# A DeltaNet attention block and a SwiGLU FFN on one core: the first group's inverse in blocks of 16 rows, corrected on TensorE

## The chip, the core and the metric

The kernel runs on one NeuronCore of a Trainium2 chip (trn2). Its time is device microseconds of one execution, as the median of several runs. A profile is one execution of its own: it gives the span from the first to the last instruction, every engine's busy time, and the clock that was granted to TensorE. Everything is float32, except that the FFN's weights arrive as 64-bit floats and are turned into float32 in the kernel by operations on their words.

## The reference

A linear recurrence over the sequence (DeltaNet), for 4 batches of 8 heads with 768 positions of 48 elements, and then an FFN over all 3072 tokens (d_model 384, d_ff 1536).

```python
def _attn_ref(q, k, v, beta):                # each (4, 8, 768, 48); beta (4, 8, 768)
    k_n = k / (np.linalg.norm(k, axis=-1, keepdims=True) + 1e-06)
    state = np.zeros((B, H, D, D))
    for t in range(S):
        kt, vt, bt = k_n[:, :, t], v[:, :, t], beta[:, :, t, None]
        y[:, :, t] = np.einsum('bhd,bhde->bhe', q[:, :, t], state)
        v_old = np.einsum('bhde,bhd->bhe', state, kt)
        state = state + bt[..., None] * np.einsum('bhd,bhe->bhde', kt, vt - v_old)
    return y

def _moe_ref(x, w_gate, w_val, w_out):        # x: y as (3072, 384)
    g = x @ w_gate
    return (g / (1.0 + np.exp(-g)) * (x @ w_val)) @ w_out
```

## The kernel before

**Chunks.** The sequence is cut into 12 chunks of 64 positions, two chunks to a group. Within a chunk the recurrence becomes matrix products. With L the strictly lower part of the 64x64 gram matrix K K^T of a head and D the diagonal of beta over the squared norms, the updates u of a chunk solve a triangular system, (I + D L) u = D r. Here r is the (scaled) v minus what the state gives for the keys. The kernel builds Z, the inverse of I + D L times D, and takes u = Z r on TensorE. Then y = Q state + P u with P the masked gram matrix of Q and K, and the state grows by K^T u. The 32 heads of a chunk lie as 2 x 16: two on the partitions (64 rows each), 16 along the free axis.

**The inverse.** It is found by substitution on VectorE for 32-row diagonal blocks of both chunks of a group at once (`substitute`, lines 524 and 530: a multiply and an add for each of 31 steps). Two 32-row blocks make the 64 rows of a chunk. The block below the diagonal comes from a join on TensorE, -Z2 L21 Z1 (`join_late` for the first two groups, lines 634 and 646).

**Order of the work.** The order on every engine is written out by hand (`tc.manual_schedule`): an engine does its instructions in program order. Group 0 is special, since nothing can lie over it. Its grams (`first_gram`: diagonal blocks and the block below), its norms (`norms`, `first_n`), `first_scale`, the substitution and `join_late(0, 0, ...)` come before chunk 0 can go. Chunk 0 is carried in five steps by `advance(0)`: r; u (line 782, copied at 793); y (lines 804, 841, 843); x by transposes (853, 856); the state (816). With x of chunk 0 the FFN starts (`gate_val`, line 1052): two 128-column blocks of gate and val are a pair, f = 0, 2, ... 10, twelve matmuls with 256 tokens moving. The pairs of chunk 0 and chunk 1 follow; `point` puts a step of the recurrence in front of a pair, `fill` puts VectorE work behind one. For chunks 0 and 1 the FFN is plain. From chunk 2 on it runs in a form with fewer products (line 957 on), which the change doesn't touch.

**Weights.** They come in pieces of 128 rows (`stage`: 256 KB for 256 columns, 512 KB for 512). ScalarE takes the words apart (`power_step`, lines 262 and 268) and VectorE puts them together (`convert`, lines 279, 287, 299). A piece is staged in a place that has no other use at the time; conversion of a piece frees its place and issues the next load. The first 12 pieces have 256 columns and cover f = 0 and 2; 12 of 512 cover the rest of gate and val; 12 follow for `w_out`. `need(n)` says that a pair needs the first n pieces.

**Queues.** Nearly all loads and stores are issued by SyncE (SP), in program order: K, Q (`load_k`, `load_q`: four issues for a chunk, 64 rows x 8 heads x 48 elements, so pieces of 192 bytes), V (`load_v`: eight issues for a chunk), weights. The first halves of K of chunks 0 and 1 also use ScalarE's queue, half of beta GpSimd's.

Of the kernel before, what the change touches and what calls it, by code (L numbers as in the profile page):

```python
# [20 lines left out]
def kernel(  # L21
# [108 lines left out]
    def halves(x, c, bp, b):  # L130
        return x[2 * bp + b, :, c * C : (c + 1) * C, :]

    def load_k(c, dmas=(nc.sync,)):
        for n in range(2 * NB):
            bp, b = divmod(n, 2)
            dmas[n % len(dmas)].dma_start(
                out=kn_of(c)[64 * b : 64 * b + 64, bp, :, 0:D],
                in_=halves(k, c, bp, b).rearrange("h p d -> p h d"),
            )

    def load_q(c):
        for bp in range(NB):
            for b in range(2):
                nc.sync.dma_start(
                    out=qpad[c % QB][64 * b : 64 * b + 64, bp, :, 0:D],
                    in_=halves(q, c, bp, b).rearrange("h p d -> p h d"),
                )
# [28 lines left out]
    def load_v(c):  # L176
        vin[c] = work.tile([128, 2, NB, NJ, D], FP32, name="vin", bufs=2)
        for bp in range(NB):
            for b in range(2):
                src = halves(v, c, bp, b).rearrange("(j par) p d -> par p j d", par=2)  # L180
                for par in range(2):
                    s = 64 * (b ^ par)
                    nc.sync.dma_start(out=vin[c][s : s + 64, par, bp], in_=src[par])
# [11 lines left out]
    for f0, m in ((0, 256), (256, 256), (512, PIECE), (1024, PIECE)):  # L195
        for t in range(KT):
            for dst, src in ((wg_sb, moe_w_gate), (wv_sb, moe_w_val)):
                pieces.append((dst, src, t, f0, m))
# [22 lines left out]
    place_of += in_wo + in_z1 + in_wo + in_work + (in_z1 + in_work) * 3  # L221

    beta_s = places["wo"].bitcast(FP32)[:, 6 * H_ : 6 * H_ + NG * 128]
    LATE = {"zb": 0, "p_sb": 6}
# [13 lines left out]
    def stage(n):  # L238
# [11 lines left out]
        nc.sync.dma_start(  # L250
# [3 lines left out]
    def power_step(n):  # L254
# [3 lines left out]
        power = words(hp[10 + (n // 2 % 4 if n < N_HALF else (0, 2, 3, 1)[n % 4])])  # L258
# [11 lines left out]
    def convert(ns):  # L270
# [24 lines left out]
        for n in range(ns[-1] + 1, ns[-1] + 7):  # L295
            if n < min(N_HALF, len(pieces)) or ns[-1] + 3 > n < len(pieces):
                power_step(n)
# [15 lines left out]
    for b in range(2):  # L313
# [9 lines left out]
        )  # L323

# [51 lines left out]
    def load_beta(at, queue=nc.gpsimd):  # L376
# [5 lines left out]
            in_=beta.rearrange("(bp b) (j par) s -> b par bp j s", b=2, par=2)[  # L382
# [13 lines left out]
    def scale_v_heads(c):  # L396
        r = vin[c].rearrange("p par bp j d -> p (par bp j) d")
        for h in range(HH):
            nc.scalar.mul(r[:, h], r[:, h], n_t[c // 2][:, c % 2, h : h + 1])

    scaled = set()

    def scale_v(c):
        scaled.add(c)
        spent.append(1.4)
        r = vin[c].rearrange("p par bp j d -> p (par bp j) d")
        n = n_t[c // 2][:, c % 2, :, None].to_broadcast([128, HH, D])
        nc.vector.tensor_tensor(out=r, in0=r, in1=n, op=ALU.mult)

    def banks(name, tag):  # L410

        if tag == "ffn":
            return [ps_ffn([128, 512], name) for _ in range(2)]
        p = ps_pair(name, tag)
        return [p[:, 0], p[:, 1]]

    def turned(c, of_q, tag=None):

        tag = tag or ("py" if of_q else "px")
# [5 lines left out]
        if c >= blocks_of[of_q][1]:  # L425
            xt_v = xt.rearrange("p (bp b j i) -> p bp j b i", bp=NB, b=2, j=NJ)
# [19 lines left out]
    def gram_steps(c, of_q, tag=None, copies=(nc.vector.tensor_copy,) * 2):  # L446

        xt = (qt if of_q else kt)[c]
        p_g = banks("p_g", tag or ("py" if of_q else "px"))
# [47 lines left out]
    z1s, mbs = {}, []  # L497
    WAIT = "wait"
# [40 lines left out]
    first_of = {}  # L539

    def first_tiles():
# [4 lines left out]
        a_sb[0] = a[:, R * R :].rearrange("p (c h j) -> p c h j", c=2, h=HH)  # L546
        zb = work.tile([128, R, R], FP32, name="zb", bufs=1)
        nc.vector.memset(zb, 0.0)
        nc.vector.memset(ztp[0], 0.0)
        first_of["zb"] = zb  # L550

    def first_gram(c, tag):

        p_g = ps_pair("p_g", tag)
        p_v = p_g.rearrange("p par (x h i) -> p par x h i", x=2, i=R)
        for bp, j, par, b, _ in every():
            k_v = kt[c][half_of(par), bp, j, b].rearrange("p (x i) -> p x i", x=2)
            h, s_ = NJ * bp + j, b ^ par
            hi, lo = slice(64 * s_, 64 * s_ + R), slice(64 * s_ + R, 64 * s_ + C)
            nc.tensor.matmul(p_v[hi, par, 1, h], k_v[:, 0], k_v[:, 0])  # L560
            nc.tensor.matmul(p_v[lo, par, :, h], k_v[:, 1], k_v)
        return p_g, p_v

    def first_diag(c, par, p, copy):
        at = HH * c + HH // 2 * par
        copy(first_of["diag"][:, at : at + HH // 2], p[1][:, par, 1])

    def first_below(c, p):
        for lo in (slice(R, C), slice(64 + R, 64 + C)):
            nc.scalar.copy(  # L570
                a_sb[0][lo, c].rearrange("p (par h) j -> p par (h j)", par=2),
                p[0][lo, :, 0 : HH // 2 * R],
            )

    def first_scale(mb, r_b):
        zb, b = first_of["zb"], beta_b[:, 0]
        nb = work.tile([128, R], FP32, name="nb", tag="nb_1", bufs=1)
        for _ in range(2):
            nc.gpsimd.tensor_tensor(out=b, in0=b, in1=r_b, op=ALU.mult)
        nc.gpsimd.tensor_copy(zb.rearrange("p k i -> p (k i)")[:, 0 : R * R : R + 1], b)  # L580
        nc.vector.tensor_scalar_mul(nb, b, -1.0)
        nc.vector.tensor_tensor(
            out=mb, in0=mb, in1=nb[:, None, :].to_broadcast([128, R, R]), op=ALU.mult
        )
        return zb
# [7 lines left out]

    def turned_m(g, tag):

        a_v = a_of[g].rearrange("p (m i) -> p m i", i=C)
        p_m = banks("p_m", tag)
        half_r = R // 2
        for j in range(R):
            p = p_m[j // half_r][:, R * (j % half_r) : R * (j % half_r) + R]  # L600
            for quad, at in QUADS:
                nc.tensor.matmul(p[quad], a_v[quad, :, at + j], ident[quad, quad])
        return [
            (slice(half_r * n, half_r * n + half_r), p.rearrange("p (j i) -> p j i", i=R))
            for n, p in enumerate(p_m)
        ]
# [50 lines left out]
    def invert(g):  # L657
# [3 lines left out]
        if g > 1:  # L661
            mb = new_mb()
            yield from turn(mb.rearrange("p j i -> p i j"), a_v[:, R:C])
        else:
            mb = mbs.pop()
# [82 lines left out]
    def advance(c):  # L748
# [7 lines left out]
        p_y = recur(ps_pair("p_y", "py"))  # L756
        if c > 0:
            p_r = recur(ps_pair("p_r", "px"))
# [20 lines left out]
        yield  # L779
        p_u = recur(ps_pair("p_u", "px"))  # L780
        for bp, j, par, b, first in every():
            nc.tensor.matmul(  # L782
                p_u[half_of(b), par, bp, j],
                zt[half_of(b ^ par), par, bp, j],
                r[half_of(b ^ par), par, bp, j],
                start=first,
                stop=True,
                skip_group_check=True,
            )
        uu = work.tile([128, 2, NB, NJ, D], FP32, name="uu", tag="r", bufs=2)  # L790
        each = range(NB) if c == 0 else (slice(0, NB),)
        for bp in each:
            nc.scalar.copy(uu[:, :, bp], p_u[:, :, bp])
# [6 lines left out]
        pq = p_sb.pop(c)  # L800

# [38 lines left out]
        for bp in each:  # L840
            nc.scalar.copy(y[:, bp, :, 0], p_y[:, 0, bp])
            for b in range(2):
                nc.scalar.copy(y[half_of(b), bp, :, 1], p_y[half_of(1 - b), 1, bp])
# [201 lines left out]
    def gate_val(c, f, fill, within=None):  # L1045

        ps = {}
        for w_sb, name in ((wg_sb, "p_gate"), (wv_sb, "p_val")):
# [11 lines left out]
            if name == "p_gate":  # L1060
                nc.scalar.activation(sil, ps[name], ACTF.Silu)
                fill(2)
                if within is not None:
                    point(within)
        new_h(c, f, len(hs))
# [496 lines left out]
```

## Time and profile before

| | |
|---|---|
| median of 3 runs | 715.93 us (715.0 to 716.48) |
| profiled execution | 713.96 us, of which the span is 712.3 us |
| mean granted TensorE clock | 0.966 |
| TensorE matmul busy | 679.6 us (95% of the span) |
| VectorE, ScalarE, GpSimd busy | 475.6, 261.8, 53.8 us |
| first FFN matmul | at 62.37 us |
| DMA over the span | 62.57 MB, mean 88 GB/s |

All places in time are microseconds from the start of the span. A line number such as L524 is the line of the kernel that issued the instruction; in a row, `out<-in` names the tiles. One float32 matmul of the program is two records in the profile (a transpose is one), so "x12" of an FFN row is six matmuls. Matmul ends are modelled, so a busy TensorE isn't one at its peak; a granted clock of 0.5 means that it runs at half its rate. "issue" as the reason of a wait means that the profile shows nothing that was waited for.

### The profile page before, as it was taken

The numbers are of one execution on the slowest core, as the hardware profiler recorded it, in microseconds if no ns is written. First come the engines' busy times: TensorE is split into PE (matmuls) and PEld (weight loads), VectorE is DVE, ScalarE is ACT, GpSimd is POOL, SyncE is SP. The second block draws the span as 40 slices with busy tenths as digits, with TensorE's granted clock in tenths as the row PEclk, the third lists the DMA queues.
The fourth block names the chain that finished last, engine by engine and source line by source line (L and its number), as shares of the span: only waits on it lengthen the run. The fifth ranks groups of instructions, "written<-read, shape, count | busy, mean of one in ns | idle before, by whom it ended". The sixth has DMA issues, their size and how long they took to land.

```text
span 712.3 us, 25668 instructions
## 1 busy us (share of the span) xinstructions
PE 679.6 (95%) x11368; PEld 637.9 (90%) x11368; DVE 475.6 (67%) x1085; ACT 261.8 (37%) x555; POOL 53.8 (8%) x46
## 2 busy tenths in 40 slices
PE   4747999999999999999999999999999999999997
PEld 3636788866799999999999999999999999999997
DVE  5995765779799967888458888469854345333342
ACT  3557755312453343224333235233153043142230
POOL 8003000201300030000120000300000000000000
PEclk9556999999999999999999999999999999999999
DMA  7786444002753162166144166035142142121210
GB/s 149 173 230 171 128 112 131 26 12 45 206 111 80 40 119 67 26 136 133 29 97 105 25 125 123 18 97 113 24 112 71 24 99 60 47 68 46 67 46 22
DMA packets 144575, 62.57 MB, mean 88 GB/s; under 512 B 124400, under 2 KB 127472, under 8 KB 144464
## 3 DMA queue, kind: packets, MB, share of 16 engines
q1 hardware_dynamic: 141968, 60.36, 36.1%
q8 instruction: 89, 1.46, 0.8%
q10 hardware_dynamic: 2112, 0.39, 0.4%
q0 software_dynamic: 384, 0.17, 0.1%
q14 instruction: 22, 0.18, 0.1%
HBM read 53.82 MB, written 7.08 MB: 86 GB/s over the span
## 4 chain that ended last, share of the span: by engine, by line
PE 89%; DVE 5%; ACT 3%; issue 1%; DMA 1%; SPq 0%; DVEq 0%; ACTq 0%
PE ffn L957 42%; PE ffn L1160 19%; PE ffn L1052 9%; PE ffn L1077 4%; PE p_g L452 3%; PE p_s L816 2%; PE p_r L760 2%; PE p_u L782 2%; DVE tmp L524 2%; DVE zb L530 2%; PE p_y L769 1%; PE p_y L804 1%; PE p_f L853 1%; DMA kn<-in_k_dram 1%; PE p_j L723 1%
## 5 line engine op out<-in xcount | busy, mean ns | idle before, releaser
L957 PE MATMUL ffn<-x_ffn,wg_sb 128*128 128x128 f32 x840 | 128.3, 275 | 0.4 <-ACT x_ffn L856 0.2
L957 PE MATMUL ffn<-x_ffn,wv_sb 128*128 128x128 f32 x840 | 128.1, 275 | 0.0
L957 PEld LDWEIGHTS ffn<-x_ffn,wg_sb 128*128 128x128 f32 x840 | 111.1, 192 | 0.7 <-ACT ffn L1013 0.3
L957 PEld LDWEIGHTS ffn<-x_ffn,wv_sb 128*128 128x128 f32 x840 | 110.7, 192 | 0.0
L987 ACT ACTIVATE sil<-ffn 128x256 f32<-128x256 f32 x120 | 46.0, 383 | 131.9 <-PE ffn L957 126.8
L1160 PE MATMUL ffn<-wo_sb,h_f 128*128 128x192 f32 x480 | 83.4, 327 | 0.0
L992 DVE TENSOR_TENSOR h_f<-sil,ffn 128x256 f32<-128x256 f32 x120 | 49.6, 418 | 47.6 <-ACT sil L987 45.1
L1160 PEld LDWEIGHTS ffn<-wo_sb,h_f 128*128 128x128 f32 x480 | 78.1, 190 | 0.4
L1121 DVE TENSOR_TENSOR ffn<-ffn,p_sb 128x512 f32<-128x512 f32 x58 | 40.4, 696 | 44.6 <-ACT ffn L1013 43.5
L530 DVE TENSOR_TENSOR zb<-zb,tmp 128x31 f32<-128x31 f32 (+15 forms) x186 | 63.7, 343 | 6.4
L524 DVE TENSOR_TENSOR tmp<-zb,mb 128x31 f32<-128x31 f32 (+15 forms) x186 | 63.2, 340 | 5.2
L957 PE MATMUL ffn<-x_t,h_f 128*128 128x128 f32 x480 | 61.2, 280 | 0.1
L957 PEld LDWEIGHTS ffn<-x_t,h_f 128*128 128x128 f32 x480 | 56.2, 191 | 1.4 <-ACT ffn L970 0.3
L668 POOL TENSOR_TENSOR n_b<-mb,half 128x32 f32<-128x32 f32 x5 | 30.0, 5995 | 297.6 <-DVE mb L494 258.5
L1121 DVE TENSOR_TENSOR o_sb<-o_sb,ffn 128x192 f32<-128x192 f32 x49 | 17.2, 351 | 51.2 <-PE ffn L1160 49.1
L970 ACT COPY ffn<-ffn 128x512 f32<-128x512 f32 x30 | 17.1, 571 | 63.6 <-PE ffn L957 57.2
L1052 PE MATMUL ffn<-x_ffn,wg_sb 128*128 128x256 f32 x144 | 35.8, 401 | 0.9 <-ACT x_ffn L856 0.9
L1160 PE MATMUL ffn<-last_k,h_f 128*128 128x192 f32 x200 | 35.9, 327 | 0.0
L1052 PE MATMUL ffn<-x_ffn,wv_sb 128*128 128x256 f32 x144 | 33.4, 381 | 0.0
L1052 PEld LDWEIGHTS ffn<-x_ffn,wg_sb 128*128 128x128 f32 x144 | 28.3, 201 | 5.6 <-ACT x_ffn L856 1.4
L1160 PEld LDWEIGHTS ffn<-last_k,h_f 128*128 128x128 f32 x200 | 32.9, 190 | 0.0
L1052 PEld LDWEIGHTS ffn<-x_ffn,wv_sb 128*128 128x128 f32 x144 | 27.0, 190 | 3.7
(242 smaller groups left out, 1048.1 us busy)
## 6 DMA issues: line engine op xcount, KB each, us to landing
h_f<-w_s SPq DMA_DIRECT2D x60, 256.0 KB
p_sb<-w_s SPq DMA_DIRECT2D x27, 256.0 KB
vin<-in_v_dram SPq DMA_DIRECT2D x96, 48.0 KB
out_dram<-o_sb SPq DMA_DIRECT2D x48, 96.0 KB
kn<-in_k_dram SPq DMA_DIRECT2D x40, 96.0 KB
zt<-in_moe_w_out_dram SPq DMA_DIRECT2D x6, 384.0 KB
qpad<-in_q_dram SPq DMA_DIRECT2D x36, 64.0 KB
wo_sb<-in_moe_w_gate_dram SPq DMA_DIRECT2D x4, 512.0 KB
```

Source lines behind the costliest of these rows:

```text
L452: nc.tensor.matmul(p_v[par][half_of(b if of_q else b ^ par), bp, j], kt[c][half_of(par), bp, j, b], xt[half_of(par), bp, j, b],)
L524: nc.vector.tensor_tensor(out=t_v, in0=zb[:, 0 : j + 1, j : j + 1].to_broadcast([128, j + 1, m]), in1=mb[:, j : j + 1, j + 1 : R].to_broad ...
L530: nc.vector.tensor_tensor(out=zb[:, 0 : j + 1, j + 1 : R], in0=zb[:, 0 : j + 1, j + 1 : R], in1=t_v, op=ALU.add,)
L668: nc.gpsimd.tensor_tensor(out=n, in0=mb.rearrange("p j i -> p (j i)")[:, 0 : R * R : R + 1], in1=half, op=ALU.pow,)
L957: nc.tensor.matmul(p[:, u], w(u), moving, start=start and u == 0, stop=True, skip_group_check=True,)
L970: nc.scalar.copy(p_y, p_x)
L987: nc.scalar.activation(sil[:, n].rearrange("p (i n) -> p i n", i=2), p[:, 0:2], ACTF.Silu)
L992: nc.vector.tensor_tensor(out=h_of(c, f, j), in0=sil[:, n].rearrange("p (i n) -> p i n", i=2), in1=p[:, 2:4], op=ALU.mult,)
L1052: nc.tensor.matmul(ps[name][:, i], w_sb[:, t, (f + i) * 128 : (f + i + 1) * 128], xts[c][:, t], start=(t == 0 and i == 0), stop=(t == KT - 1),
L1077: nc.tensor.matmul(p_o, hs[c, f - f % 2][:, f % 2, bp * 128 : (bp + 1) * 128], wo_sb[:, f], start=(f == 0), stop=(f == FT - 1),)
L1121: nc.vector.tensor_tensor(out=out, in0=a, in1=b, op=ALU.add)
L1160: nc.tensor.matmul(p[x, part], a(f - f % 2)[:, f % 2], b(f), start=not begun and f == 0, stop=f == FH - 1, skip_group_check=True,)
```

## The change

The first group's inverse is made differently, and what hangs on it is put in another order.

- **Blocks of 16 rows.** The substitution of group 0 runs on 16-row diagonal blocks, the two of a 32-row part at once in one instruction: 15 steps. Nothing is joined. What results is Z for block-diagonal matrices of 16 rows.
- **Three rounds.** With L now the part below the 16-row blocks, N = -D' L (D' for Z of the blocks) is made on TensorE (`n_products`), and u follows from v0 = Z r by three times u = v0 + N u: products on TensorE, sum on VectorE. N has no entries but below the blocks, so three rounds are exact for four blocks. L is masked by ScalarE with per-row factors (`low_gram`, `low_copies`, and masks `m_rows`, `m_low`, made by VectorE from the identity); Z is spread from 16-row blocks to its places with masks too (`spread_z`).
- **Loads.** The batches that share a row pair are chosen differently (0 with 2 and 1 with 3 instead of 0 with 1 and 2 with 3), so that 16 heads of a half lie behind each other in memory: K and Q take two issues for a chunk, V four. The first two weight pieces go to ScalarE's queue, the others come behind Q0, K2, K3 and V0.
- **Pieces.** Gate and val have 24 pieces of 256 columns and 6 of 512; staging places and the pace of conversion change with them. Pieces 0 and 1 are converted beside the first norms.
- **Order.** v of chunks 0 and 1 is scaled on GpSimd. Q of chunk 1 and its gram come before the substitution ends. Chunk 1's chain (state, r, v0, three rounds, state, y, x) is put between the matmuls of the first two pairs, one step behind every three matmuls (`behind`). The inverse of group 1 begins after the first pair of chunk 1, with its own transposes on VectorE instead of TensorE's (`turned_m` goes).

The core of the diff:

```diff
-        for bp in range(NB):
-            for b in range(2):
-                nc.sync.dma_start(
-                    out=qpad[c % QB][64 * b : 64 * b + 64, bp, :, 0:D], ...
+    def load_heads(t, x, c, dmas=(nc.sync,)):
+        for b in range(2):
+            dmas[b % len(dmas)].dma_start(
+                out=t[64 * b : 64 * b + 64, :, :, 0:D].rearrange("p bp h d -> p (bp h) d"),
+                in_=halves(x, c, b).rearrange("bp h p d -> p (bp h) d"))
...
-    for f0, m in ((0, 256), (256, 256), (512, PIECE), (1024, PIECE)):
+    for f0, m in ((0, 256), (256, 256), (512, 256), (768, 256), (1024, PIECE)):
...
+    def low_gram(c, bank):
+        p_g = banks("p_g", bank)
+        ...
+        for bp, j, par, b, _ in every():
+            k_v = kt[c][half_of(par), bp, j, b]
+            nc.tensor.matmul(p_v[par][half_of(b ^ par), bp, j], k_v, k_v)
+        return p_g
+    def low_copies(c, p_g):
+        for par in range(2):
+            ...
+            for x in range(3):
+                at = slice(B16 * x, B16 * x + B16)
+                nc.scalar.mul(l_sb[c][:, HH // 2 * par : HH // 2 * (par + 1), at],
+                              p_h[:, :, at], m_low[:, x : x + 1])
...
+    def first_substitution():
+        zb, mb = pairs_of_blocks(first_of["zb"]), pairs_of_blocks(first_of["mb"])
+        for j in range(B16 - 1):
+            m = B16 - 1 - j
+            ...   # t_v: 2 * (j + 1) * m elements
+            nc.vector.tensor_tensor(out=t_v, in0=zb[...], in1=mb[...], op=ALU.mult)
+            nc.vector.tensor_tensor(out=z_v, in0=z_v, in1=t_v, op=ALU.add)
+    def spread_z(c, x, engine): ...          # 128 x 512, by engine
+    def n_products(c, p_n, bp):
+        for j in range(NJ):
+            for par, b in ORDER:
+                rows, h = half_of(b ^ par), HH // 2 * par + NJ * bp + j
+                nc.tensor.matmul(p_v[par][half_of(b), bp, j], l_sb[c][rows, h], zt[rows, h])
...
     def advance(c):
+        for bp in range(NB):
+            if c == 0:
+                n_products(c, p_n, bp)
+                n_copies(c, p_n, bp, nc.scalar.copy)
+            p_u_of(bp, lambda par, bp, j: zt[:, par, bp, j], r, lambda b, par: half_of(b ^ par))
+            if c == 0:
+                nc.scalar.copy(v0[:, :, bp], p_u[:, :, bp])
+        if c > 0:
+            nc.scalar.copy(v0, p_u)
+        uu = v0
+        if c < 2:
+            yield MORE
+            for n in range(3):
+                for bp in range(NB):
+                    p_u_of(bp, lambda par, bp, j: n_m[:, par, NJ * bp + j],
+                           uu if n else v0, lambda b, par: half_of(b))
+                    if c == 0:
+                        plus(uu[:, :, bp], v0[:, :, bp], p_u[:, :, bp])
+                if c > 0:
+                    plus(uu, v0, p_u)
+                    if n < 2:
+                        yield MORE
...
-        for n, _ in enumerate(substitute(mb, zb)):
-        ...
-        m_1 = turned_m(1, "ffn")
-        scale_v_heads(0)
-        first_join = join_late(0, 0, ("px", "py"))
+        scale_v(0, nc.gpsimd)
+        scale_v(1, nc.gpsimd)
+        for c in range(2):
+            low_copies(c, low_gram(c, 2 * c))
+        ...      # q0, k2, k3, q1: transposes and grams
+        first_substitution()
+        first_z()
+        spread_z(0, 0, nc.vector)
+        spread_z(0, 1, nc.scalar)
+        step("advance", advance, 0)
+        ...
+        def chain(at):
+            step("advance", advance, 0 if steps("advance", 0) < 4 else 1)
+            converts(1 + (at + 1) % 2)
-            need((6, 12, 18, 18, 24, 24)[f // 2])
-            gate_val(c, f, fill, 1 if early else None)
+            need((6, 12, 18, 24, 30, 30)[f // 2])
+            gate_val(c, f, fill, at, chain if early else None)
```

## The prediction, made before the changed kernel ran

> **What bounds the kernel now.** I read the page's first two parts first: who is busy, and when.
>
> ```profile
> PE 679.6 (95%) x11368; PEld 637.9 (90%) x11368; DVE 475.6 (67%) x1085; ACT 261.8 (37%) x555; POOL 53.8 (8%) x46
> PE   4747999999999999999999999999999999999997
> PEclk9556999999999999999999999999999999999999
> ```
>
> TensorE is busy 95% of the span, and nearly all its idle time and its whole loss of clock lie in the first five slices of 17.8 us. The engines' busy time by stage says the same in numbers (columns: window, its length, busy us and count per engine, granted clock, DMA share, GB/s):
>
> ```profile
> 0.00:20.00 20.00, 10.03 (x281) 8.01 (x282) 12.18 (x20) 8.07 (x15) 14.46 (x28) 0.89 0.72 146
> 20.00:44.00 24.00, 15.34 (x472) 12.89 (x472) 21.77 (x64) 11.82 (x36) 0.00 (x0) 0.57 0.83 237
> 44.00:62.00 18.00, 10.38 (x326) 8.61 (x326) 14.64 (x40) 13.66 (x36) 5.26 (x1) 0.50 0.55 116
> 62.00:79.00 17.00, 15.20 (x320) 12.38 (x324) 11.87 (x22) 13.96 (x25) 0.36 (x1) 0.86 0.79 233
> 79.00:190.00 111.00, 110.66 (x1533) 87.15 (x1525) 81.79 (x180) 44.27 (x87) 13.95 (x8) 1.00 0.31 80
> 190.00:712.00 522.00, 517.95 (x8453) 508.87 (x8451) 333.37 (x763) 169.98 (x362) 19.73 (x9) 1.00 0.34 75
> ```
>
> From 79 us TensorE is the bound. Before the first FFN matmul it isn't: from 20 to 44 us VectorE is busy 21.8 of 24 us and TensorE works beside it. The order of time names the chain:
>
> ```profile
> 20.34 0.19 DVE L524 TENSOR_TENSOR tmp<-zb,mb 128x31 f32<-128x31 f32 x1
> ...
> 22.49 0.30 DVE L524 TENSOR_TENSOR tmp<-zb,mb 128x135 f32<-128x135 f32 x1
> ...
> 43.45 0.21 DVE L530 TENSOR_TENSOR zb<-zb,tmp 128x31 f32<-128x31 f32 x1
> 43.69 1.92 DVE L610 STREAM_TRANSPOSE zt<-zb 128x1024 f32<-128x1024 f32 x1
> 45.51 1.21 DVE L616 STREAM_TRANSPOSE p_sb<-zb 128x1024 f32<-128x1024 f32 x1
> ...
> 53.53 1.73 PE L782 MATMUL p_u<-vin,zt 64*64 64x48 f32 x52 [0.15 <-ACT zt L654]
> ...
> 62.37 5.03 PE L1052 MATMUL ffn<-x_ffn,wg_sb 128*128 128x256 f32 x12 [0.95 <-ACT x_ffn L856]
> 79.64 2.86 PE L1052 MATMUL ffn<-x_ffn,wv_sb 128*128 128x256 f32 x12
> ```
>
> So: substitution 20.3 to 43.7, transposes to 46.7, joining of the blocks to 53.5, u, y, and x at 62.4, where the FFN begins. Anything that brings 62.4 forward moves the whole end, unless the stage after it can't follow.
>
> [...] 12 FFN matmul records took 5.03 us at 62 us and 2.86 at 80, and the granted clock was 0.50 from 44 to 62. [...] TensorE's unexplained "issue" waits (2.7 us at 12.7, 3.9 at 36.9) fall where the DMA share was about 1. [...] GpSimd idles from 20 to 56 us.
>
> **The change, part by part.** Times are those of the trace before.
>
> *Up to the substitution (20.34).* VectorE gets six small operations for the row masks between the two norms (0.2 us each by its 128x32 rows, 1.2 in all) and the memset after them now waits for the first weight piece; the second GpSimd power (ends 15.7) starts some 0.7 later. Converting pieces 0 and 1 (four ScalarE at 0.33, six VectorE, 1.9) fits beside those powers. The scaling of mb has 512 elements instead of 1024: 0.69 (the 128x512 row) for 1.23. Start: 20.34 + 0.7 - 0.5 = 20.5. SP: two K issues fewer, so beta's eight (0.73 each) start 1.5 earlier; Q0, K2, K3 lose the four weight pieces ahead of them. The first two pieces go to ScalarE's queue (two issues of 0.43 behind its table load, idle there until 7.5).
>
> *Substitution.* Fifteen steps instead of 31, over both blocks at once, with 30 to 128 elements. Start to start an operation takes 0.23 at 31 elements and 0.33 at 135, so 0.20 + 0.001 each: 30 x 0.20 + 2 x 1360 x 0.001 = 8.7 instead of 23.4. End: 29.2.
>
> *To Z.* One transpose of 1024 with one strided side (1.2 to 1.9 by the two rows above: 1.6) and the mask multiply, halved between VectorE and ScalarE (0.6): 31.4. Gone: a second transpose and the join. GpSimd now scales v of chunks 0 and 1 beside the substitution: 768 elements, two inputs each. [...] I take 1: 32.4.
>
> *TensorE's own queue up to there.* After the first grams (16.4) it has two full grams, 32 transposes and four grams. At half clock (2.0 per 64 records, 1.95 per 8 transposes) 2 x 2 + 4 x 1.95 + 4 x 1.95 = 19.6, to 36; at full clock half of it, then ScalarE's copies (3.6 for twelve masked ones, 6.4 for the others) pace it to 29. Q of chunk 1 is needed at about 25. An issue took 0.66 to 0.92 us whether it had 256 or 512 row pieces, so I give the double ones 0.9; pieces of 192 B moved at 112 GB/s at 0.66 of the DMA (170 to 190 at full), weights at 350 to 410. K0 to K3, Q0, V0, Q1 and six pieces then land by 25. So N = -DL begins at 33 (31.5 to 37).
>
> *N, v0, three rounds, y, x.* Cold: N and v0, 128 records at 0.031 with the ScalarE copies between, 4.0; three rounds of 64 records, 6, and the last sum (0.6) and handovers, 0.7; p_y 2.0; y on two engines 1.3 (1.95 on ScalarE before); transposes and x 2: 16. Warm, 11. I take 15, since before the clock stayed at 0.50 here: the FFN starts at **48** (42 to 54), 14.4 earlier. Pieces 2 to 5 are converted behind y, 4 x 1.03, the first two just in time.
>
> *After that.* TensorE loses the second join (0.7 + 1.9) and the gram of q1 (1.1) and gains three rounds for chunk 1 (3 x 1.08): **-0.5**. But chunk 1's chain now goes through its queue with only three matmuls (six records, 1.4 us) between steps. Its answer is 0.95 on VectorE plus 0.3 handover, and conversions of one or two pieces (1.03, 2.06) stand ahead: VectorE has ten conversions (10.3), three sums, r and the state (0.95 each) and two products (0.69), with the shared passes some 17 us, against 20 of TensorE (eight FFN slots of 1.39, nine small products), so waits of about half a us, twice or thrice; the copy of v0 is behind sixteen ScalarE powers (5.3), another 0.6; the pieces of f = 6 (three per fill, 3.1) come 1.6 late. With the cold start (1.8) that is some 5.6 lost until f = 6. Before, from 62.4 to 78.5, 16.2 us held 12.1 of work (three FFN groups of 2.8, one of 1.1, 2.6 of joining), so 4.1 were lost. Difference: **+1.5**. Cover: DMA has 24 pieces and the chunks, about 10 MB, done in 45 us at the 237 GB/s shown above; f = 6 is at 84. The inverse of group 1 starts one fill later and its turns move to VectorE (2 x 1.1), so the last join slides into the last outputs, and y of chunk 2 has nothing over its copies (1.44): **+1.5**. Other moved issues and halved V loads: 0, TensorE is continuous above them. That batches pair differently changes no count.
>
> **Sum.** -14.4 - 0.5 + 1.5 + 1.5 = -11.9: span 712.3 to 700.4. The profiled execution took 713.96 with its 1.7 around the span, 2.0 under the median of the runs; so 702.1 for a like one, and 704.0 beside the median of 715.93.
>
> **Rivals.**
> - *Warm and free of contention:* Z at 31.4, TensorE at full clock through the rounds, FFN at 42.5. For: before, the clock was 1.00 at 30 to 32 after dense grams. Against: 0.50 from 34 on. -19.9 + 2.5: **698.5**. Chance 0.20.
> - *N held up:* Q of chunk 1, instruction waits or a cold queue keep TensorE until 40. For: 3.9 us of such a wait at 37. Against: fewer and earlier issues. 7 later: **711**. Chance 0.15.
> - *Only moved:* weights or conversions hold the FFN at the old place, gain within 0.2%: **716**. Against: ScalarE and VectorE had 3 and 5 us to spare from 62 to 79, and the pieces are converted in the same order. Chance 0.04.
> - *Slower, by the ramp:* in chunk 1's eight slots a convert or the powers stand before each answer and each costs 2 us, 16, with 2 for f = 6: -14.4 - 0.5 + 18 + 1.5 = +4.6, **720.5**. It decides once waits between the first FFN matmul and f = 6 pass 19 us (5.6 expected). For: VectorE some 85% full there. Against: its conversions can slip, and TensorE's four PSUM banks let it run ahead. Chance 0.09.
> - *As summed:* 0.52, its own range 700 to 709.
>
> 0.2% is 1.4 us, about what a measurement of this kernel can tell from no change. Faster: 0.52 + 0.20 + 0.15 = 0.87; same 0.04; slower 0.09. The range, 697 to 712, takes in the first two rivals.
>
> **What would show it.** Right: about 15 pairs of operations in the first substitution ending at 29 to 31, the first FFN matmul at 45 to 51, VectorE no longer solid from 20 to 44, TensorE idle about 12 less in all. Wrong: first FFN matmul after 54; TensorE's waits on VectorE sums or on ScalarE's copy of v0 over 10 us; more than 3 us lost where chunk 2 begins; a substitution row slower than 0.33 at 128 elements [...].

## The result: slower, and the profile after

The changed kernel takes 727.04 us (median of 4 runs, 722.88 to 728.84) where the kernel before took 715.46 beside it (714.43 to 716.48): a ratio of 1.0154, 95% interval 1.0108 to 1.02. Run again later it took 724.85 (723.03 to 726.28), ratio 1.0147, interval 1.0127 to 1.0168. The forecast was 704.0. Its profiled execution took 726.94 us, with a span of 725.2.

The page of the changed kernel, its first two parts (busy time; the span in 40 slices of 18.1 us):

```profile
PE 690.6 (95%) x11368; PEld 650.0 (90%) x11368; DVE 470.3 (65%) x1091; ACT 259.7 (36%) x552; POOL 55.4 (8%) x49
PE   4678999999899999999999999999999999999997
PEclk9956999999899999999999999999999999999999
```

The clock is low in the third and fourth slices (before: second to fourth), and slice 11, near 190 us, is new: TensorE is partly idle there, and at a lower clock. TensorE is "busy" 11 us longer with the same number of records (11368). Busy time by stage, the stages of the forecast (window, its length, busy us and count of PE, PEld, DVE, ACT, POOL, clock, DMA share, GB/s):

```profile
20.00:44.00 24.00, 16.61 (x496) 15.46 (x496) 14.69 (x38) 13.10 (x30) 3.27 (x3) 0.86 0.91 224
44.00:62.00 18.00, 12.63 (x299) 11.76 (x296) 4.96 (x12) 4.44 (x12) 0.00 (x0) 0.62 0.42 115
62.00:79.00 17.00, 15.27 (x336) 12.30 (x338) 9.65 (x29) 12.03 (x34) 0.00 (x0) 0.80 0.14 25
79.00:190.00 111.00, 108.45 (x1234) 85.02 (x1234) 89.51 (x207) 48.31 (x93) 15.36 (x7) 1.00 0.37 96
190.00:725.00 535.00, 528.13 (x8683) 517.06 (x8674) 339.09 (x777) 174.70 (x370) 23.12 (x12) 0.99 0.34 77
```

VectorE is no longer the solid engine of 20 to 44 (14.7 of 24 us, before 21.8), as forecast. But from 44 to 62 every engine has room, TensorE with 12.6 of 18 us at a clock of 0.62 included: a chain of waits, not an amount of work. Below, the same places as in the forecast's order of time, for VectorE and then ScalarE and TensorE (start, length, engine, line, names, shapes, count, and in brackets the wait in front and who ended it):

```profile
22.95 1.43 DVE L634 TENSOR_TENSOR tmp<-zt,wo_sb 128x110 f32<-128x110 f32 x1
24.41 0.27 DVE L640 TENSOR_TENSOR zt<-zt,tmp 128x110 f32<-128x110 f32 x1
...
30.45 0.21 DVE L640 TENSOR_TENSOR zt<-zt,tmp 128x30 f32<-128x30 f32 x1
30.70 2.02 DVE L644 STREAM_TRANSPOSE mb<-zt 128x1024 f32<-128x1024 f32 x1
32.76 0.66 DVE L657 TENSOR_SCALAR zt<-mb,m_rows 128x512 f32<-128x512 f32 x1
```

```profile
36.63 1.07 ACT L495 COPY a_sb<-p_g 128x512 f32<-128x512 f32 x2 [3.66 <-PE p_g L469]
37.59 1.18 ACT L655 ACTIVATE zt<-mb,m_rows 128x512 f32<-128x512 f32 x1
...
31.65 0.86 PE L469 MATMUL p_g<-last_k 64*64 64x64 f32 x42
35.66 0.81 PE L469 MATMUL p_g<-last_k 64*64 64x64 f32 x19 [3.15 <-issue]
38.83 1.13 PE L666 MATMUL p_n<-zt,a_sb 64*64 64x64 f32 x32 [0.54 <-ACT zt L655]
43.15 1.14 PE L865 MATMUL p_u<-v,qpad 64*64 64x48 f32 x32 [0.60 <-ACT v L892]
45.01 1.48 PE L865 MATMUL p_u<-v,qpad 64*64 64x48 f32 x32 [0.73 <-DVE uu L1247]
47.16 1.95 PE L865 MATMUL p_u<-uu,qpad 64*64 64x48 f32 x32 [0.67 <-DVE uu L1247]
49.77 1.94 PE L865 MATMUL p_u<-uu,qpad 64*64 64x48 f32 x32 [0.66 <-DVE uu L1247]
63.70 2.93 PE L1176 MATMUL ffn<-x_ffn,wg_sb 128*128 128x256 f32 x6 [0.95 <-ACT x_ffn L979]
```

The substitution ends at 30.66 instead of 43.7, and VectorE's half of Z is there at 33.4. All of that is gone again at 63.70, where the FFN starts (before: 62.37). N begins at 38.8 only, and from 43.15 the three rounds go one half round at a time, each half waiting for the sum of the other half: 14.3 us up to the products of y at 57.45.

By stages, from marks that both traces have (first FFN matmul, first output matmul, first matmul on x of chunk 2, end), in us of span time:

| stage | before | after | difference | forecast |
|---|---|---|---|---|
| start to first FFN matmul | 62.37 | 63.70 | +1.3 | -14.4 |
| to first output matmul | 84.25 | 88.97 | +4.7 | +1.0 |
| to first matmul of chunk 2 | 41.90 | 45.84 | +3.9 | +1.5 |
| to the end | 523.8 | 526.7 | +2.9 | 0 |
| span | 712.3 | 725.2 | +12.9 | -11.9 |

So 24.8 us are to be explained: 15.7 in the start, 3.7 in the pairs of chunks 0 and 1, 5.3 at and behind chunk 2's boundary.

How far one trace can be trusted shows in a second trace of the changed kernel, from the later runs. Its stages are 64.63, 87.81, 45.70 and 526.4. N begins at 36.06 there, 2.8 us earlier, and the rounds still begin at about the same time (42.78 for 43.15) and take longer (15.6 for 14.3), as the clock is 0.50 all through. The time of an execution goes with its mean clock: of the eight executions of this kernel the slowest had 0.966 (728.84 us), and 0.979 and 0.986 had 722.88 and 723.03. So differences of about 1 us in one stage of two traces mean little here.

The traces say more of what the profile calls "issue". If all instructions of TensorE in a trace are counted in order of time (weight loads, matmuls and those of its sequencer), all 76 such waits over 0.25 us in the 14 traces begin after 449 instructions or a multiple of 256 more (12 of them one later), and each ends 1.2 to 1.7 us after a packet of 16 KB landed on the queue that the profile names "instruction". So I read them as waits for the next 256 of TensorE's own instructions; the forecast left them unexplained. The places keep to that count; the length changes from run to run (behind instruction 1218 it is 3.15 us in the changed kernel's first trace and 0.50 in its second).

### The profile page after: what moved, and what is told of

It reads as the page before. It is cut to its first block, busy times and chain, and to the rows that moved or that the text cites. A ratio compares the mean times of both kernels' runs of the same rounds, so it can differ in the third digit from the quotient of the medians.

```text
span 725.2 us, 25577 instructions
## 1 busy us (share of the span) xinstructions
PE 690.6 (95%) x11368; PEld 650.0 (90%) x11368; DVE 470.3 (65%) x1091; ACT 259.7 (36%) x552; POOL 55.4 (8%) x49
## 4 chain that ended last, share of the span: by engine, by line
PE 63%; DVE 1%; ACT 0%; issue 0%; DVEq 0%; ACTq 0%
PE ffn L1080 37%; PE ffn L1286 17%; PE p_g L469 2%; PE p_u L865 1%; PE p_r L840 1%; PE p_y L926 1%; PE p_s L938 1%; PE p_y L849 1%; PE p_f L976 1%; PE p_j L803 1%; PE p_j L817 1%; DVE tmp L541 0%; DVE zb L547 0%; DVE o_sb L1247 0%; DVE kt L444 0%
## 5 line engine op out<-in xcount | busy, mean ns | idle before, releaser
L1247 DVE TENSOR_TENSOR ffn<-ffn,p_sb 128x512 f32<-128x512 f32 x58 | 40.3, 695 | 40.6 <-ACT ffn L1136 39.4
L547 DVE TENSOR_TENSOR zb<-zb,tmp 128x31 f32<-128x31 f32 (+15 forms) x155 | 53.1, 343 | 5.3
L541 DVE TENSOR_TENSOR tmp<-zb,mb 128x31 f32<-128x31 f32 (+15 forms) x155 | 52.7, 340 | 4.2
L748 POOL TENSOR_TENSOR n_b<-mb,half 128x32 f32<-128x32 f32 x5 | 29.2, 5838 | 332.4 <-DVE mb L511 332.4
```

Source lines behind the costliest of these rows:

```text
L541: nc.vector.tensor_tensor(out=t_v, in0=zb[:, 0 : j + 1, j : j + 1].to_broadcast([128, j + 1, m]), in1=mb[:, j : j + 1, j + 1 : R].to_broad ...
L547: nc.vector.tensor_tensor(out=zb[:, 0 : j + 1, j + 1 : R], in0=zb[:, 0 : j + 1, j + 1 : R], in1=t_v, op=ALU.add,)
L748: nc.gpsimd.tensor_tensor(out=n, in0=mb.rearrange("p j i -> p (j i)")[:, 0 : R * R : R + 1], in1=half, op=ALU.pow,)
L1247: nc.vector.tensor_tensor(out=out, in0=a, in1=b, op=ALU.add)
```

## The experiments

Each is the changed kernel with one edit, unless said otherwise. The ratios are to the kernel before, run beside them (714.2 to 715.1 us); the changed kernel stands at 1.015 on that scale, and 0.001 is 0.7 us.

**e1: the quadrants of TensorE.** A round multiplies a 64x64 block of N with a 64x48 block of u for each head (2j + par), each pair of batches (bp) and each of the two batches of the pair (b, which is also the half of the 128 rows that holds its block).

```diff
-                        p_u[half_of(b), par, bp, j],
+                        p_u[half_of(b ^ par), par, bp, j],
```

The edit is for the rounds only.

> Only the places of the rounds' products change: those of par = 1 go to the other half of the rows, so that the four 64x64 quadrants of TensorE take turns instead of the two on the diagonal. (The products are added to the wrong half, so what is computed is not the update; instruction counts, shapes and waits are those of the changed kernel.) Theory 'the diagonal halves the rate': 64 records of a round take 1.15 us instead of 2.07 at full clock (chunk 1), and a half round of chunk 0 at half clock 1.05 to 1.15 instead of 1.95. That is 6 x 0.85 = 5.1 off the start of the FFN (63.7 to 58.6) and 3 x 0.9 = 2.7 off chunk 1's rounds, some 7.8 us in all: 719. Rival 'the rate is that of loading a new weight tile for every product, or of the clock': 2.07 and 1.95 stay, 727.

Measured: 719.96 us, ratio 1.0064 (1.0043 to 1.0086). A round of chunk 1, from the order of time of the changed kernel, then of e1:

```profile
77.51 2.07 PE L865 MATMUL p_u<-v,zb 64*64 64x48 f32 x64
```

```profile
73.41 1.15 PE L865 MATMUL p_u<-v,zb 64*64 64x48 f32 x64
```

The diagonal nearly halves the rate, as the first theory said; the rounds of chunk 0 take 11.3 instead of 14.3 us. A quadrant is here a pair of the half of the rows that is read and the half that is written. With "read half b, write half b" only two of the four are ever used, with the edit all four, and 64 records take 1.15 us instead of 2.07, a factor of 1.8.

**e2: their order.** The same two quadrants, but b goes 0, 1, 0, 1 in the rounds instead of 0, 1, 1, 0.

```diff
-                for par, b in ORDER:
+                for par, b in ((0, 0), (1, 1), (1, 0), (0, 1)):
```

> Only the order of the rounds' products changes: halves 0, 1, 0, 1 instead of 0, 1, 1, 0, so that no quadrant is used twice in a row; the two on the diagonal remain the only ones used. Theory 'two quadrants are the limit': 64 records stay at 2.07 us at full clock, half rounds at 1.95, time 727 within 1. Rival 'a repeat of the same quadrant is what stalls': 2.07 becomes about 1.2 and the time goes down by some 7 us, to 720.

Measured: 726.5 us, ratio 1.0172 (1.0131 to 1.0213); 2.07 and 1.94 to 1.95 (at half clock) stay. So a repeat of one quadrant is not what costs; the number in use is (1.15 us with four in e1, 2.07 with two here).

**e3: halves by PSUM bank.** For chunk 0; a half is 32 records either way.

```diff
-                for bp in range(NB):
...
-                    plus(uu[:, :, bp], v0[:, :, bp], p_u[:, :, bp])
+                for par in range(2):
...
+                    plus(uu[:, par], v0[:, par], p_u[:, par])
```

> Chunk 0's rounds are split by par (each par has a PSUM bank of its own) instead of by bp (each half lies in both banks). Theory 'a half round waits for the other half's sum because they share the banks': the five waits of 0.66 us between half rounds go, half rounds follow each other in 1.95 instead of 2.61, so the FFN starts 3.3 us earlier (60.4) and the time is 3 us lower, 724. Rival 'the wait is the chain itself (product, sum, product)': half rounds stay 2.6 us apart, 727.

Measured: 724.03 us, ratio 1.0117 (1.0067 to 1.0166), and in its order of time the waits are where they were:

```profile
50.90 1.95 PE L906 MATMUL p_u<-uu,qpad 64*64 64x48 f32 x32 [0.67 <-DVE uu L1260]
53.51 1.95 PE L906 MATMUL p_u<-uu,qpad 64*64 64x48 f32 x32 [0.67 <-DVE uu L1260]
```

The bank theory is out: half rounds stay 2.61 us apart. The median is somewhat lower, but the intervals overlap.

**e4: no rounds for chunk 0.**

```diff
-            uu = new_u("uu")
-            for n in range(3):
+            uu = new_u("uu") if c else v0
+            for n in range(3 if c else 0):
```

> Chunk 0's three rounds and their sums are left out (u of chunk 0 is v0, so the result is not the reference's); N is still made, and chunk 1 keeps its rounds. It moves the start of the FFN alone. The rounds took 43.2 to 57.5, so the FFN should start at about 49.5 instead of 63.7. Theory 'what the start gains, the end gains': 14 us less, 713. Rival 'the ramp gives it back' (weights not yet there or not yet converted, chunk 1's chain): TensorE's idle time between the first FFN matmul and f = 6 grows from 2.5 us to 8 or more and the time falls by 8 or less, 719 to 725.

Measured: 714.78 us (20 runs), ratio 1.001 (0.9995 to 1.0024), so 10 to 12 us less. The FFN starts at 51.31, 12.4 earlier, and the output at 137.46, 15.2 earlier. What the start gains, the end gains. And the other side of it: with the FFN 11 us earlier than in the kernel before, the time is that of the kernel before. The later stages lose the whole.

**e6: a PSUM tile for each half.** As e3, with the products of each par in a tile of its own, a new one in each round.

```diff
+                    p_1 = [recur(ps_ffn([128, 1, 512], "p_u", par))[:, 0] for par in range(2)]
-                        plus(uu[:, par], v0[:, par], p_u[:, par])
+                        plus(uu[:, par], v0[:, par], p_1[par])
```

> As e3 (chunk 0's rounds split by par), but the products of par 0 and par 1 go to two PSUM tiles of their own, instead of the two banks of one tile. In e3 the waits of 0.66 us stayed. Theory 'the order between the halves is kept for the whole tile of the products': with two tiles the wait goes where the sum of the other half alone was waited for; half rounds follow in 1.95 to 2.0 instead of 2.61, the rounds end 3 us earlier, the FFN starts 3 us earlier and the time falls by 3 us, to about 724. Rival 'the order is kept by the tile that the sums write (u), or the handover itself takes 0.66': half rounds stay 2.6 us apart, time 727.

Measured: 718.45 us (14 runs), ratio 1.0047 (1.003 to 1.0063). In its order of time the waits for the sums are gone; the second and third rounds are one block:

```profile
51.06 6.24 PE L910 MATMUL ffn<-uu,qpad 64*64 64x48 f32 x123
```

So the order between the halves had been kept for the tile, whatever the bank (0.67 us of wait in front of each half round shown for e3, none inside these 6.24 us). The gain is two to three times what I expected (6 us beside the changed kernel's later runs), and the clock is the likely reason. Four rows of busy time, each over the rounds of chunk 0: the changed kernel, e6, and the two kernels below with an earlier N, e8 with the waits and e10 without them:

```profile
43.15:57.45 14.30, 10.91 (x223) 10.14 (x226) 3.24 (x6) 4.66 (x10) 0.00 (x0) 0.59 0.58 166
```

```profile
45.73:57.68 11.95, 10.28 (x235) 10.22 (x229) 2.94 (x6) 5.28 (x12) 0.00 (x0) 0.55 0.54 150
```

```profile
38.98:54.56 15.58, 12.19 (x223) 11.38 (x226) 3.24 (x6) 4.66 (x10) 0.07 (x1) 0.50 0.78 210
```

```profile
38.23:46.54 8.31, 7.39 (x233) 7.22 (x229) 2.95 (x6) 5.33 (x12) 1.48 (x1) 0.87 0.94 248
```

The last two rows show what the waits do to the clock. N begins at 34.5 in both and the clock is 0.50 in front of the rounds; with the waits it stays there through all 15.6 us, without them it is full from about 40.3 (mean 0.83 from 40 to 41, 1.00 from 41 to 45), and the rounds take 8.3 us, with the same two quadrants. Of the 7.3 us between them 2.5 are idle time and 4.8 are work at a higher clock. In e6's profiled execution, the slowest of its 14, TensorE stood still once (1.67 us, for instructions) and the clock came only at 56.5 (0.50 up to 56, 0.76 from 56 to 57); its fastest executions had a mean clock of 0.992 (714.02 and 714.66 us), this one 0.971.

**e7: the inverse of group 1 one fill earlier.**

```diff
-        for _ in range({1: 2, 2: 3}.get(g, 4)):
+        for _ in range({1: 1, 2: 3}.get(g, 4)):
             yield WAIT
```

> One wait step of the inverse of group 1 is left out (one fill waited for instead of two), so that its substitution, the join and chunk 2's chain each begin one fill earlier; TensorE's order in the output stage is then that of the kernel before, with two of its matmuls over the copies of y. Theory 'chunk 2's boundary lost its cover': TensorE's idle time of about 2 us at 191 to 196 goes, so does the half clock behind it, and the time from the first output matmul to chunk 2's first FFN matmul falls from 45.8 to about 42.5, with 1.5 less just behind it: 4 to 5 us less, 722.5. Rival 'VectorE can't be earlier': TensorE waits in an earlier place for Z of group 1 instead, and the time stays within 1 of 727.

Measured: 718.31 us (18 runs), ratio 1.0046 (1.0025 to 1.0066). TensorE at the boundary, order of time: the changed kernel, then e7:

```profile
190.18 1.56 PE L1203 MATMUL ffn<-wo_sb,last_h 128*128 128x384 f32 x4
...
193.27 1.14 PE L926 MATMUL p_y<-uu,p_sb 64*64 64x48 f32 x62
196.03 1.54 PE L976 MATMUL p_f<-ident,y 128*128 128x128 f32 x6 [1.62 <-ACT y L966]
...
198.51 1.22 PE L1080 MATMUL ffn<-x_ffn,wg_sb 128*128 128x128 f32 x4
```

```profile
191.39 1.11 PE L926 MATMUL p_y<-uu,p_sb 64*64 64x48 f32 x64
192.43 1.56 PE L1203 MATMUL ffn<-wo_sb,last_h 128*128 128x384 f32 x4
194.12 0.88 PE L976 MATMUL p_f<-ident,y 128*128 128x128 f32 x6
...
195.89 0.71 PE L1080 MATMUL ffn<-x_ffn,wg_sb 128*128 128x128 f32 x4 [0.21 <-ACT x_ffn L979]
```

In the changed kernel the last output matmuls stand ahead of the y products, nothing lies over the copies of y, and what follows runs at half clock (0.50 from 196 to 202 us): p_f 1.54 instead of 0.88, the FFN's first four records 1.22 instead of 0.71. In e7 two output matmuls (four records) lie over the copies. From first output matmul to chunk 2's first: 41.92 us, as before the change; from there to the end 523.7, as before. The first theory holds, with some 7 us instead of 4 to 5. It doesn't rest on this trace alone: the four traces with the earlier inverse (e7, e10, e11, e12) have 41.9 and 523.7 us in these two stages, the nine others of the changed kernel and its variants 44.5 to 46.3 and 525.4 to 527.5.

**e8: N first.**

```diff
-        turned(1, True, 0)
         gram(2, False, "px", (copy_a, copy_a))
-        gram(3, False, "py", (copy_a, copy_a))
-        first_q.append(gram_steps(1, True, 0)); next(first_q[1])
+        turned(1, True, 0)
...
         n_products(1, p_n, 1)
+        first_q.append(gram_steps(1, True, 0)); next(first_q[1]); next(first_q[1])
...
         def chain(at):
             step("advance", advance, 0 if steps("advance", 0) < 4 else 1)
+            if grams:
+                gram(grams.pop(), False, "py", (copy_a, copy_a))
```

So the gram of q1 stands behind chunk 0's y products, and that of k3 (`grams` holds a 3) in the first call of `chain`.

> The gram of k3 and that of q1 no longer stand ahead of N in TensorE's and ScalarE's queues: q1's comes behind chunk 0's y products, k3's behind the first FFN matmuls; the transposes of q1 stand behind the gram of k2. Theory 'N was late because ScalarE's half of spreading Z stood behind k3's copies, and those behind TensorE's': N begins at 34 to 35 instead of 38.8, the FFN 2.5 to 4.5 us earlier (59.5 to 61, as q1's gram at half clock is now between y's products and x), and the time falls by 3 to 4 us, 723.5. Rival 'TensorE's stalls without a visible cause only move': N at 38 or later, 727.

Measured: 720.2 us, ratio 1.0082 (1.0068 to 1.0096), some 5 us less. The first theory holds:

```profile
34.49 1.13 PE L666 MATMUL p_n<-zt,a_sb 64*64 64x64 f32 x32 [1.80 <-DVE p_sb L487]
...
60.85 1.97 PE L1176 MATMUL ffn<-x_ffn,wg_sb 128*128 128x256 f32 x6 [0.95 <-ACT x_ffn L979]
```

N begins 4.3 earlier, the FFN 2.9, and the end follows. Beside the second trace of the changed kernel N is only 1.6 earlier, but the rounds begin at 38.98 instead of 42.78 and the FFN is 3.8 earlier. What the theory leaves out is TensorE's own queue: in the changed kernel it ended with the gram of q1 at 38.28, so ScalarE alone held N for 0.54 (1.3 in the second trace). The edit shortens both queues, and this run doesn't tell their shares apart.

**e9: twice the issues.**

```diff
-            dmas[b % len(dmas)].dma_start(out=t[64 * b : 64 * b + 64, :, :, 0:D]..., in_=...)
+            for bp in range(NB):
+                dmas[b % len(dmas)].dma_start(out=t[64 * b : 64 * b + 64, bp, :, 0:D], in_=...[bp]...)
```

`load_v` likewise.

> The third part of the change undone alone: K and Q take four issues for a chunk and V eight again, with the pairing of batches and the order of loads kept. Ahead of Q1 there are 13 more issues on SP at 0.65 to 0.9 us, partly in time that SP waits for room anyway. Theory 'SP's issues set when Q1 and V1 land': Q1 lands 4 to 9 us later than 29.7, N and the FFN come 3 to 7 us later, 730 to 734. Rival 'the bytes set it': Q1 lands within 1 us of 29.7, 727.

Measured: 724.59 us (720.21 to 727.02), ratio 1.0133 (1.0108 to 1.0158). Q1 does land later, TensorE's transposes of it are at

```profile
36.85 1.94 PE L455 MATMUL ffn<-ident,qpad 128*128 128x128 f32 x8 [11.85 <-DMA qpad<-in_q_dram]
```

and N begins at 44.33, 5.5 later than in the changed kernel. But the FFN is 3.9 later, the output 2.7, chunk 2's first matmul 1.4, the end 0.1, and the runs show no difference that can be told. So the forecast of 730 to 734 failed. Half the issues do bring N forward. Of what was lost at N, 1.0 comes back by the rounds, which begin 4.5 later and whose first three half rounds take 1.14, 1.13 and 1.65 us instead of 1.14, 1.48 and 1.95; the 1.2 to 1.3 that each later stage gives back are no more than traces of kernels with the same later stages differ (see e7). Single executions of these kernels differ by some 3 us either way, as much as this. Why the median of the runs doesn't show the later start, while e4, e8 and e10 do show an earlier one, is open.

**e10: the edits of e6, e7 and e8 together.**

> The edits of e6, e7 and e8 together, nothing left out: chunk 0's rounds with a PSUM tile for each par, one fill less before the inverse of group 1, the grams of k3 and q1 behind N. If each removes a loss of its own place (start of the rounds 4.3 earlier, rounds 3.3 to 4 shorter, output stage 3.9 and the cold restart behind it 1.5 to 3 shorter), the FFN starts at 56 to 57, the output at 144 to 145, chunk 2's first matmul at 186 to 187, and the time is 712 to 714, against 714.4 of the kernel before. If one loss takes the place of the other (the ramp up to f = 6 gives back what the start gains), the time is 717 or more.

Measured: 708.61 us (706.55 to 710.54), ratio 0.992 (0.9901 to 0.9939): faster than the kernel before. N at 34.55, FFN at 52.97, output at 140.55, chunk 2 at 182.47. The three gains add up: beside the changed kernel's later runs e6, e7 and e8 gain 6.4, 6.5 and 4.7 us, 17.6 together, and e10 gains 16.2. The FFN starts 3 to 4 us earlier than forecast, since the rounds, without waits, come to full clock (mean 0.87 over them, see e6).

**e11: e10 with four quadrants in earnest.** For par = 1 the products land in the other half of the rows, and VectorE adds across; in chunk 0 each bp has a tile of its own.

```diff
+                                p_u[half_of(b ^ par), par, bp, j],
...
+                    plus(uu[:, 0, at], v0[:, 0, at], p_at[:, 0])
+                    for b in range(2):
+                        plus(uu[half_of(b), 1, at], v0[half_of(b), 1, at], p_at[half_of(1 - b), 1])
```

> As e10, and the rounds use all four quadrants of TensorE: the products of par = 1 land in the other half of the rows, and VectorE adds them across (two sums of 64 rows for par = 1, one of 128 for par = 0); chunk 0's halves are by bp, each with PSUM tiles of its own; both chunks so. Nothing is left out. TensorE: 64 records in 1.15 instead of 2.07 (3.9 to 2.1 at half clock). VectorE: a half round has sums of 0.38 + 2 x 0.36, about 1.1, instead of 0.56, so chunk 0's half rounds should follow each other in 1.2 instead of 1.95: rounds 4 to 4.5 shorter than in e10, chunk 1's rounds 2.7 less of TensorE, of which VectorE's longer sums (1.6 for 0.95) may take half: 5.5 to 7 less than e10, 706 to 708. Rival 'the sums across the halves are slow or become the bound': within 2 of e10.

Measured: 708.75 us, ratio 0.9921 (0.9905 to 0.9938), no difference from e10. For chunk 0 the rival was right: a round's six sums take 2.28 to 2.36 us with 0.15 between, VectorE is the bound, TensorE waits for it (0.17 to 0.55) and stays at a clock of 0.50 (up to 54 us), so the rounds take 8.6 us. For chunk 1 the quadrants pay: 1.15 for 2.07, and the stage from FFN to output is 84.86 instead of 87.58 us (in e10 with one wait of 1.1 for instructions, here with 1.6 us of waits for VectorE's longer sums).

**e12: the best of each.** Chunk 0's rounds as in e10, chunk 1's as in e11, and the transposes of q1 behind ScalarE's half of spreading Z.

> The parts that did best, nothing left out: chunk 0's rounds as in e10 (by par, a PSUM tile each), chunk 1's as in e11 (four quadrants), one fill less before the inverse of group 1, the grams of k3 and q1 behind N, and the transposes of q1 with their copies behind ScalarE's half of spreading Z. In e11 the stage from the first FFN matmul to the output took 84.9 us against 87.6 in e10, while chunk 0's rounds took as long (8.6 and 8.3, counted to the y products). So if the two are additive: 708.6 - 2.7 - 0.5 to 1 for an earlier N = 705 to 705.5. If chunk 1's longer sums only fit because e11's FFN starts later (55.6 against 53.0), 708 to 709.

Measured: 706.29 us (705.59 to 707.19), ratio 0.9879 (0.9859 to 0.9899), 8.8 us less than the kernel before and about 1 more than the two parts would give. Its stages of busy time (rounds of chunk 0; FFN to output; output to chunk 2; the rest):

```profile
37.66:44.95 7.29, 6.95 (x233) 6.88 (x229) 2.94 (x6) 5.36 (x12) 1.48 (x1) 0.89 1.10 266
54.40:139.47 85.07, 82.29 (x1150) 70.07 (x1151) 67.47 (x161) 55.18 (x116) 10.26 (x6) 1.00 0.37 111
139.47:181.39 41.92, 41.74 (x680) 26.60 (x678) 37.24 (x90) 8.95 (x17) 9.18 (x3) 1.00 0.34 79
181.39:705.10 523.71, 519.39 (x8465) 510.36 (x8462) 335.48 (x767) 171.69 (x364) 19.74 (x9) 1.00 0.34 75
```

The last two stages are those of the kernel before to 0.1 us, the second is 0.8 above it, and the start is 8.0 below (54.40 for 62.37): the forecast's shape, with a start 6.4 short of the 48 forecast. Part of that is one wait for instructions, behind which TensorE was slow again up to the transposes of y (the gram of q1 took 2.01 us, in e10 1.15; the six transposes 1.14, in e10 0.87):

```profile
49.77 0.81 PE L666 MATMUL ffn<-zt,a_sb 64*64 64x64 f32 x20 [3.11 <-issue]
```

## Why the prediction was wrong

- **Substitution, end 29.2: right but for one multiply.** It began at 20.85 for 20.5 and ended at 30.66. The row said it: 0.29 us at 128 elements, and one multiply of 110 elements took 1.43 instead of 0.27, exactly while GpSimd scaled v of chunk 0 (22.76 to 24.25). That is 1.16 more, once and not twice, as v of chunk 1 landed only at 38.2. I had taken 1, my own estimate, for which no trace of the kernel before had a case. Z, at 32.4, was 33.4 on VectorE: the strided transpose took 2.02, not 1.6.
- **N at 33: wrong by 5.8.** This is the rival "N held up" (until 40), which I gave 0.15, and two of its reasons are there. Q of chunk 1 landed at 29.7, not by 25, and TensorE waited 1.68 us for it. Then TensorE's gram of k3 stood still for 3.15 us in its middle, for instructions. So TensorE's queue, which I had ending at 29 to 36, ended at 38.28. The last half a us is a wait that I had not in the sum: ScalarE's half of spreading Z stood behind the copies of k3's gram, and those behind that gram. I had ScalarE's copies as the pace of TensorE's queue, but not as something that Z stands behind. e8 took k3 and q1 out of the way: N at 34.5.
- **Three rounds in 6.7: the step that failed, at 14.3.** Both terms of the sum were too small. I priced the products at 2.0 us for 64 records at half clock, 6 in all, from rows that use four quadrants, where the rounds use two (e1: a factor of 1.8; e2): TensorE worked 10.9 us, 4.9 more (12.2 in the second trace, where the clock is 0.50 all through). And I allowed 0.7 for the last sum and all handovers, where five waits of 0.66 to 0.73 stood between the half rounds, 3.4 us, because the program keeps order for a tile (e3 against e6). That is 2.7 more, 7.6 with the price. The clock is no part of the 7.6, as I had counted half clock already. But cold or warm, 16 or 11, was the right question: I took the clock as given by the trace before, and the new chain's own gaps decide it (0.50 with the waits in e8, 0.87 without them in e10).
- **FFN at 48: 63.70.** N 5.8, rounds 7.6, y and x 1.0 (6.25 for 5.3), v0 0.3, and the 1 us that I took off the cold sum: 15.7.
- **"TensorE -0.5": it was about +2.2.** The same price: chunk 1's rounds cost 3 x 2.0, not 3 x 1.08, +2.7. e1 and e11 take it out again. For the ramp the forecast of 1.5 is near by luck: 4.7 in the stage, less 2.2, is 2.5 (1.4 in the second trace), but its parts are others. TensorE idled 2.5 us from 63.70 to 96.17, of which 2.0 were two waits for instructions and 0.4 one for ScalarE's copy of x. The waits for VectorE's sums and for the copy of v0 that I had counted didn't occur, and neither did the rival "slower by the ramp", which needed 19 us of waits up to f = 6.
- **Chunk 2's boundary +1.5: right in kind, 3.9 in size,** with nothing allowed for what follows. That the inverse starts one fill later and y has nothing over its copies is what the trace shows and e7 undoes. But I priced only the copies (1.44; the wait for them is 1.62). Two waits of the join for ScalarE's copies, 0.78 together, and one of 0.36 for instructions come on top, and some 1.1 is work at half clock: behind the gaps it was 0.50 from 196 to 202 us. Of the 2.9 behind the boundary 1.5 is half clock too (the first 40 records of the FFN take 6.5 us instead of 5.0), and 0.7 is one wait of TensorE for VectorE's transposes of keys at about 315 us. The rest isn't placed, but all of it hangs on the boundary: in e7 that stage took 523.7, as before.
- **"Anything that brings 62.4 forward moves the whole end": right.** e4, e8 and e10 show it; e9 alone does not.
- The list of what would show it wrong had the right places: first FFN matmul after 54, more than 3 us lost where chunk 2 begins. It had no line for the length of a round.

## What to carry to other kernels

Price a small matmul from a row that reads and writes the same halves of the array: the same 64 records cost 1.15 or 2.07 us by that alone (e1). Where a product and its sum take turns in halves, give each half a tile of its own and look in the trace whether the waits are gone; the clock that short waits hold down can cost more than the waits (4.8 and 2.5 us between e8 and e10). And when a part is moved, follow each engine that makes a piece of the result, not only the busiest: here ScalarE's 1.2 us stood behind a copy that stood behind a gram that could have come 25 us later (in e10 it begins at 56.04, not 31.65).

## What the runs showed of the hardware that I had not expected

- The way to full clock differed from run to run. With 64x64 products without gaps TensorE had full clock about 5.3 us after their start in e12 (from 33.98; its mean clock from 39 to 40 is 0.87, so the step from 0.5 lies near 39.3), and by the same reading after 5.8 in e10 (from 34.55; 0.83 from 40 to 41) and 6.6 in e6 (from 49.84; 0.76 from 56 to 57). What sets the time isn't shown.
- The clock was lost with short gaps alone. In the changed kernel it was 1.00 from 44 to 45 us and 0.50 from 46 to 47, and it stayed there to 59, though no gap of TensorE from 38.83 to 57 was longer than 0.73 us. In e8, with gaps of 0.60 to 0.73 us between half rounds of 1.95, it never left 0.50 from 38.98 to 54.56.
- TensorE stood still for its own instructions, as read in the section on the result: 76 waits over 0.25 us in the 14 traces, each behind the 449th instruction or a multiple of 256 more (12 of them one later) and each ended 1.2 to 1.7 us after a packet of 16 KB landed. The longest took 3.9 us (the kernel before, at 36.9).
- VectorE adds operands from different halves of the rows, SBUF and PSUM, without a penalty to be seen: in e11 three sums of 384 columns, two of them across the halves, took 1.69 us, 0.56 each, and in the changed kernel a sum of 384 columns with all operands in the same rows took 0.56.
- GpSimd's elementwise product of 128x768 took 1.49 us, and a VectorE product of two SBUF inputs that began 0.19 after it ended only 0.13 after it (1.43 us instead of 0.27). Beside GpSimd's second product (38.18 to 39.65) VectorE's products with one input in PSUM took 0.68 and 0.69 us, as without it (0.68).
